# A recurrent-attention, two-MLP kernel: its first MLP group in float32 worked per chunk of 128 tokens, its bonus vector loaded by rows, its step order recomputed

## The chip, the cores and the metric

The kernel runs on one core of one Trainium2 chip. The metric is the device time in microseconds (us) of one execution; 359.74 us is the median of three runs of the kernel before (359.56 to 360.32). One execution was also taken with the hardware profiler; its trace is what the rows below come from.

## What is computed

The reference, cut to its three stages. `r`, `k`, `v`, `w` are [2, 8, 768, 48], all float32:

```python
def _attn_ref(r, k, v, w, u):              # recurrence over t, per batch and head
    for t in range(S):
        cur = einsum('bhd,bhe->bhde', u * k[t], v[t])
        y[t] = einsum('bhd,bhde->bhe', r[t], state + cur)
        state = w[t][..., None] * state + einsum('bhd,bhe->bhde', k[t], v[t])

def _moe_ref(x, g_ln, w_ch1, w_ch2):       # x: [2, 768, 384]; w_ch1 384x1536, w_ch2 1536x384
    xn = (x - mean) / sqrt(var + 1e-06) * g_ln
    return x + maximum(xn @ w_ch1, 0) @ w_ch2

def _moe2_ref(x, w_in, w_spatial, b_spatial, w_out):
    h = maximum(x @ w_in, 0); u, v = halves of h
    v_s = einsum('ts,bsd->btd', w_spatial, layer_norm(v)) + b_spatial[None, :, None]
    return (u * v_s) @ w_out
```

The weights arrive as float64, and the kernel makes float32 of them on the chip.

## The kernel before

The 768 tokens of each of the two batches are cut into 6 chunks of 128, so there are 12 chunks, numbered i = 2c + b. Each chunk goes through the attention in chunked form: `prep` (decay scans and products on VectorE), `keys_t` (transposed keys), `scores`, `values`, `state`, `norm` (layer norm statistics, a ScalarE square root, a normalized `xn`), and `turned`, which transposes `x` and `xn` and copies them out of PSUM: `x` to `x2v`, `xn` to `xfirst` (float32) for chunks 0 and 1, and to a float16 high part and low part in a ring (`xring_h`, `xring_l`) for the others.

The first MLP works on groups of two chunks, 256 token columns: `moe1(g)` for g = 0 to 5. For each of the 12 slices f of 128 hidden units, `up(f)` multiplies the weights `w1` with the 256 columns, ScalarE applies the relu (`hi`), and `down(f)` multiplies `w2` into three accumulators. Group 0 uses the float32 weights `w1f` and `w2f` directly. Groups 1 to 5 use float16 high and low parts (`w1h`, `w1l`, `w2h`, `w2l`) in three products each. The 24 weight pieces (`w1_piece`, `w2_piece`, 384 KB of float64 words each) are loaded on SP's queue, and each needs a shift, a rebias on ScalarE, a sign step and a merge on VectorE (`convert`, lines 549 to 608, the merge being line 590) before it is `w1f` or `w2f`; the copy to the high part and the subtraction for the low part come later. After the attention, stage 2 (`v_tile`, `u_tile`, `sp_tile`, `o_tile`) computes the second MLP.

Every instruction is a step `add(engine, cost, key, fn, r, w)`. A planner inside the kernel (class `Plan`) runs a list schedule over these steps with the costs written there: whenever an engine is free, it takes the ready step with the lowest key. The result is a fixed order of instructions for each engine. The keys come from the constants in `PP` (line 56). So `PP` decides the order, and at run time each engine goes through its own list in order and waits at any instruction whose input isn't there. Where the planner sees TensorE waiting it puts in matmuls on a zero tile, `pw<-warm`, which compute nothing that is used. It does so only up to the first step that writes the PSUM bank `acc0`, which is a `down` of group 0.

PSUM banks are handed out in rotation by tag (`bank(tag)`): two banks for `up`, two for `acc`. Where a helper issues every operation, all have its line: `mm` is line 394, `cp` line 385, `sub` 388, `mul` 391.

The bonus vector `u` of 384 numbers is also needed as `ud`, [112, 8], one column per head, with the 48 values of the head down the partitions. `set_ud` clears it on GpSimd, and `load_u` (line 525) fills it with two DMAs that pick single elements of `u`. They stand on SP's queue between the token loads of chunk 0 and chunk 1.

Of the kernel before, what the change touches and what calls it, by code (L numbers as in the profile page):

```python
# [8 lines left out]
F32 = mybir.dt.float32  # L9
# [12 lines left out]
DM = H * D  # L22
# [320 lines left out]
@with_exitstack  # L343
def tile_rwkv_moe_gmlp(ctx: ExitStack, tc: tile.TileContext, dt_in, tok_in, vg_in, u_in, g_in, w1_in, w2_in, win_in, wsp_in, b_in, wout_in, out, plan_only=False):
    nc = tc.nc
# [124 lines left out]
    def load_d(i, key):  # L470
        c, b = divmod(i, B)
        s = i % 2

        def part(lo, hi, first):
            def fn():
                if first:
                    t["dt", i] = a2.tile([R, DTC], F32, tag=f"dt{i % 2}", name=f"dt{i}")
                Q.dma_start(out=t["dt", i][:, lo:hi], in_=dt_in[b, c, :, lo:hi])  # L478
            return fn

        if i < B:
            for n, (lo, hi, w) in enumerate(((2 * NP * C, DTC, "dw"), (NP * C, 2 * NP * C, "dk"), (0, NP * C, "dr"))):
                add("D", 750, key + 0.01 * n, part(lo, hi, not n), w=[(w, s)])
        else:
            add("D", 2250, key, part(0, DTC, True), w=[("dw", s), ("dk", s), ("dr", s)])

    def load_k(i, key):
        c, b = divmod(i, B)
        n = DM if i < NU else 3 * DM

        def fn():
            k = t["tk", i] = share.tile([128, 3 * DM], F32, tag=f"tk{i % 2}", name=f"tk{i}")
            Q.dma_start(out=k[:, 0:n], in_=tok_in[b, c, :, 0:n])

        add("D", 640 * n // DM, key, fn, w=[("tv", i % 2), ("tr", i % 2)])

# [37 lines left out]
    add("G", 508, -80, set_mask, w=["mask"])  # L534
    add("G", 42, -95, set_ud, w=["ud"])
    for b in range(B):
# [205 lines left out]
    def scores(i):  # L742
        s = i % 2
        pp = [bank("sc"), bank("sc")]
        ams = [slot("am", AB), slot("am", AB)]

        def sc():
            q_ = [pst(pp[j], f"sc{i}_{j}") for j in range(2)]
            t["sc", i] = q_
            for pr in range(NP):  # L750
                for j, (lo, hi) in enumerate(halves):
                    mm(q_[j][:, C * pr:C * pr + C], t["kt", i][lo:hi, pr], t["rt", i][lo:hi, pr], True, True)

# [6 lines left out]
        add("T", 1090, ka(i, "sc"), sc, r=[("E", s), ("G", s), "att"], w=pp, use=0.42)  # L760
        for j in range(2):
            add("V", cv(512), ka(i, "am"), masked(j), r=[pp[j], "mask", "att"], w=[ams[j]], two=False)
        t["amt", i] = ams

    def values(i):
# [168 lines left out]


    def moe1(g):
        o = (B * g) % RING * C
        n = B * C
        qs = [(B * g + j) % RING for j in range(B)]
        xr = [(a, q) for a in (("xh", "xl") if g else ("xf",)) for q in qs]  # L940
        xh, xl = xring_h[:, :, o:o + n], xring_l[:, :, o:o + n]
# [6 lines left out]
        def up(f):  # L948
            sl = slice(128 * f, 128 * f + 128)
            p = bank("up")  # L950
            hh, hl = slot("hh" if g else "hf", 3), slot("hl", 3) if g else None
            hts[f] = hh, hl

            def mm_():
                z = t["up", g, f] = pst(p, f"pup{g}_{f}_")
                if not g:
                    for k in range(KD):
                        mm(z[:, 0:n], w1f[:, k, sl], xfirst[:, k], k == 0, k == KD - 1)
                    return
                mm3(z[:, 0:n], [(w1h[:, k, sl], w1l[:, k, sl], xh[:, k], xl[:, k]) for k in range(KD)])  # L960

            def hi():
                hs[f] = [hp.tile([128, n], F16 if g else F32, tag=f"{hh[0]}{hh[1]}", name="hh")]
                A.activation(out=hs[f][0], in_=t["up", g, f][:, 0:n], func=ACTF.Relu)
# [4 lines left out]

            add("T", 9 * ch(256) if g else 3 * 430, ku(g, f), mm_, r=[*([("w1h", f), ("w1l", f)] if g else [("w1", f, "f")]), *xr], w=[p])  # L970
            add("A", ca(256, True), ku(g, f) - PP["EV"], hi, r=[p], w=[hh])
            if not g:
                hts[f] = (hh,)
                return
            add("V", cv(256), ku(g, f) - PP["EV"], lo, r=[p, hh], w=[hl], two=False)

        def down(f):
            def mm_(d):
                def fn():
# [3 lines left out]
                    sl = slice(128 * d, 128 * d + 128)  # L983
                    first, last = f == 0 and d != 1, f == KH - 1 and d > 0
                    if not g:
                        mm(acc(d), w2f[:, f, sl], hs[f][0], first, last)
                        return
                    hh, hl = hs[f]
                    mm3(acc(d), [(w2h[:, f, sl], w2l[:, f, sl], hh, hl)], start=first, stop=last)
                return fn  # L990

            for d in range(KD):
                w = at if f == 0 and d == 0 else [at[d // 2]]
                add("T", 3 * ch(256) if g else 430, ku(g, f + 1) + 0.01, mm_(d), r=[*([("w2h", f), ("w2l", f)] if g else [("w2", f, "f")]), *hts[f]], w=w)
# [7 lines left out]
        xv = x2v.rearrange("q k (b c t) -> q k b c t", b=B, t=C)[:, :, :, g]  # L1002
        k = ku(g, KH) - PP["EV"]
        x2 = [("x2", B * g + j) for j in range(B)]

        def plus(z, y):
            V.scalar_tensor_tensor(out=z, in0=y, scalar=W_UP ** -2, in1=z, op0=ALU.mult, op1=ALU.add)

        add("V", cv(512), k, lambda: plus(xv[:, 0:2], t["acc", g, 0].rearrange("q (k b t) -> q k b t", k=2, b=B)), r=[at[0]], w=x2, two=False)
        add("V", cv(256), k, lambda: plus(xv[:, 2], acc(2).rearrange("q (b t) -> q b t", b=B)), r=[at[1]], w=x2, two=False)  # L1010

# [6 lines left out]
    for i in range(NCH + 1):  # L1018
# [12 lines left out]
        if i == 1:  # L1031
            t["pwt"] = bank("acc")
            for f in range(KH):
                key = PP["CV"] + PP["CS"] * f
                for j, piece in enumerate((w1_piece, w2_piece)):
                    n = 2 * f + j
                    piece(f, (key + PP["CW"] * j, 0.01), lo_eng="V", sh=who("SH", n), sg=who("SG", n), later=PP["HK"] + PP["HS"] * f + PP["HW"] * j)
        if i >= 2 and i % 2 == 0:
            moe1(i // 2 - 1)
    T2 = mstart(NC)  # L1040
# [309 lines left out]
def _pack(r, k, v, w, u, moe_g_ln, moe_w_ch1, moe_w_ch2, moe2_w_in, moe2_w_spatial, moe2_b_spatial, moe2_w_out):  # L1350
# [48 lines left out]
```

## Time and profile before

| what | us |
|---|---|
| median of 3 runs | 359.74 |
| the profiled execution, its own time | 362.65 |
| its span, first to last instruction | 360.9 |
| TensorE busy (matmuls, filler included) | 351.7 |
| of that, filler `pw<-warm`, 259 matmuls | 19.0 |
| VectorE busy | 283.6 |
| ScalarE busy | 155.3 |
| mean granted TensorE clock, share of full speed | 0.991 |

PE is TensorE, PEld its weight loads, DVE VectorE, ACT ScalarE, POOL GpSimd, SP SyncE, whose queue (SPq) issues the DMAs. A matmul's shown duration includes its latency, and matmuls overlap; what one costs in a full stream is read from the distance between starts. A float32 matmul shows as two instructions. `pup` is the PSUM tile that `up` writes, numbered anew for each f.

### The profile page before, as it was taken

To read this page: it belongs to the slowest core of one execution; us is meant where nothing else is said; L and a number is where in the kernel's file an instruction comes from. 1 tells how busy PE (TensorE), PEld (TensorE's weight loads), DVE (VectorE), ACT (ScalarE), POOL (GpSimd) and SP (SyncE) were. 2 spreads that over 40 slices of the span, in tenths; PEclk is the share of its full clock that TensorE was granted. 3 is DMA by queue.
4 is the path that set the end of the run, shared out by engine and by line. 5 is a ranking of instruction groups with operands and counts; after the bars stand their busy time and mean duration, and the time that the engine had idled before them with its cause. 6 is when DMAs were issued, how large, how long until landed. Compare 5 with 4: busy or idle time off the path is not lost.

```text
span 360.9 us, 7549 instructions
## 1 busy us (share of the span) xinstructions
PE 351.7 (97%) x3041; PEld 298.8 (83%) x3041; DVE 283.6 (79%) x675; ACT 155.3 (43%) x364; POOL 2.2 (1%) x22
## 2 busy tenths in 40 slices
PE   8989999999999999999999999999999999999992
PEld 8989887779888888888889888889765899965692
DVE  7969999999999999999999999999255783025500
ACT  1557988333232332423544765663421354211121
POOL 1000000000000000000000000000000000000000
PEclk9989999999999999999999999999999999999998
DMA  8999796132222541320101026601000000210021
GB/s 211 295 307 360 232 312 201 33 112 67 77 67 78 145 129 41 119 67 31 59 31 60 30 74 200 194 3 44 3 2 0 2 0 2 79 54 2 0 84 58
DMA packets 13022, 34.85 MB, mean 97 GB/s; under 512 B 1840, under 2 KB 3888, under 8 KB 12976
## 3 DMA queue, kind: packets, MB, share of 16 engines
q1 hardware_dynamic: 12976, 34.26, 30.4%
q8 instruction: 26, 0.43, 0.5%
q14 instruction: 20, 0.16, 0.1%
HBM read 31.90 MB, written 2.36 MB: 95 GB/s over the span
## 4 chain that ended last, share of the span: by engine, by line
PE 89%; DMA 7%; ACT 1%; SPq 1%; issue 0%; DVE 0%; ACTq 0%
PE p L394 34%; PE acc L394 21%; DMA raw<-in_w 5%; PE sc L394 3%; DMA tk<-in_tok 2%; PE kT L717 1%; SPq L478 1%; PE pup__641 L394 0%; PE y__996 L394 0%; PE pup__930 L394 0%; PE pup__804 L394 0%; PE pup__1051 L394 0%; PE pup__981 L394 0%; PE pup__845 L394 0%; PE pup__773 L394 0%; PE pup__750 L394 0%
## 5 line engine op out<-in xcount | busy, mean ns | idle before, releaser
L394 PE MATMUL acc<-hh,w2h 128*128 128x256 f16 x180 | 49.2, 273 | 0.0
L394 PE MATMUL acc<-hl,w2h 128*128 128x256 f16 x180 | 49.1, 273 | 0.0
L394 PE MATMUL acc<-hh,w2l 128*128 128x256 f16 x180 | 49.1, 273 | 0.0
L394 PE MATMUL p<-ws,vn 128*128 128x384 f16 x288 | 47.1, 326 | 0.0
L394 PEld LDWEIGHTS <-vn 128*128 128x128 f16 x288 | 28.0, 98 | 18.7 <-issue 0.4
L394 PEld LDWEIGHTS <-w2h 128*128 128x128 f16 x360 | 33.9, 98 | 6.3 <-issue 2.2
L394 PEld LDWEIGHTS <-w1h 128*128 128x128 f16 x360 | 34.9, 98 | 4.3 <-issue 0.2
L1224 DVE SCALAR_TENSOR_TENSOR misc<-p,misc 128x384 f32<-128x384 f32 x16 | 8.9, 558 | 30.6 <-PE p L394 30.6
L385 ACT ACTIVATE gh<-misc 128x384 fp32r<-128x384 f32 x16 | 8.4, 523 | 41.2 <-DVE misc L1225 41.2
L568 ACT ACTIVATE raw<-raw 128x384 f32<-128x384 f32 (+1 forms) x40 | 20.8, 524 | 4.3 <-DMA raw<-in_w 4.3
L574 ACT ACTIVATE raw<-raw 128x384 uint32<-128x384 uint32 (+1 forms) x31 | 15.9, 512 | 11.9 <-DMA raw<-in_w 11.9
L585 DVE SCALAR_TENSOR_TENSOR raw<-raw 128x384 int32<-128x384 int32 (+1 forms) x40 | 20.2, 511 | 0.4 <-ACT raw L568 0.3
L394 PE MATMUL pw<-warm 128*128 128x128 f16 x259 | 19.0, 242 | 1.1 <-DVE warm L499 1.1
L394 PEld LDWEIGHTS <-w2l 128*128 128x128 f16 x180 | 17.6, 98 | 2.1
L394 PEld LDWEIGHTS <-w1l 128*128 128x128 f16 x180 | 17.6, 98 | 2.1
L394 PEld LDWEIGHTS <-warm 128*128 128x128 f16 x259 | 18.0, 111 | 1.2 <-DVE warm L499 1.1
L394 PE MATMUL acc<-hh,w2f 128*128 128x256 f32 x72 | 17.9, 385 | 0.0
L388 DVE TENSOR_TENSOR gl<-misc,gh 128x384 fp32r<-128x384 f32 x16 | 8.9, 558 | 9.4 <-ACT gh L385 9.4
L394 PE MATMUL p<-woh,gl 128*128 128x384 f32 x48 | 16.3, 340 | 0.0
L394 PE MATMUL p<-woh,gh 128*128 128x384 f32 x48 | 16.2, 337 | 0.0
L394 PE MATMUL p<-xh,winh 128*128 128x384 f32 x48 | 16.2, 337 | 0.0
L394 PE MATMUL p<-wol,gh 128*128 128x384 f32 x48 | 16.1, 336 | 0.0
(702 smaller groups left out, 911.4 us busy)
## 6 DMA issues: line engine op xcount, KB each, us to landing
raw<-in_w SPq DMA_DIRECT2D x24, 384.0 KB, 7.2
dt<-in_dt SPq DMA_DIRECT2D x10, 675.5 KB, 5.3
tk<-in_tok SPq DMA_DIRECT2D x10, 576.0 KB, 3.7
raw<-in_win SPq DMA_DIRECT2D x12, 256.0 KB, 3.1
raw<-in_wsp SPq DMA_DIRECT2D x6, 384.0 KB, 3.4
out<-misc SPq DMA_DIRECT2D x12, 192.0 KB, 1.9
raw<-in_wout SPq DMA_DIRECT2D x4, 384.0 KB, 3.4
dt<-in_dt SPq DMA_DIRECT2D x4, 224.0 KB, 5.2
```

Of the source, the lines that this page charges most:

```text
L385: A.activation(out=out, in_=in_, func=ACTF.Copy)
L388: eng[e].tensor_tensor(out=out, in0=in0, in1=in1, op=ALU.subtract)
L394: T.matmul(out=out, lhsT=lhsT, rhs=rhs, start=start, stop=stop)
L478: Q.dma_start(out=t["dt", i][:, lo:hi], in_=dt_in[b, c, :, lo:hi])
L568: A.activation(out=e, in_=e, func=ACTF.Copy, scale=REBIAS * 2 if whole else REBIAS)
L574: A.activation(out=z, in_=z, func=ACTF.Copy, scale=TOP3, bias=TOP3_BIAS)
L585: V.scalar_tensor_tensor(out=lw, in0=hw, scalar=SIGN, in1=lw, op0=ALU.bitwise_and, op1=ALU.bitwise_or)
L717: T.transpose(pv[:, j, 0:R], t["kt", i][:, j], ident[0:R, 0:R])
L1224: add("V", cv(384), key, lambda: V.scalar_tensor_tensor(out=tm_(), in0=t["spp", b, th, f][:, 0:384], scalar=1.0 / S_UP, in1=t["b"][:, ts], ...
```

## The change

- `moe0` takes the place of `moe1(0)`. Its `up(f, j)`, its relu and its three `down(f, j)` are done for each of the two chunks j on 128 columns, where `moe1(0)` did both on 256. `up(f, j)` needs only `xfirst` of chunk j. The two chunks add into the same accumulators. The relu results have four buffers (`hf`), where they had three. As `bank("up")` is called for j = 0 and j = 1 in turn, each chunk has one of the two `up` banks. The steps for j = 0 have keys of their own (`E0`, `E0S`), which are lower than nearly all others.
- `moe1(g)` for g = 1 to 5 issues the same instructions as before.
- `ud` comes laid out as [112, 8] from the host (`in_ud`) in one DMA. The two DMAs of `load_u` by single elements and the clearing on GpSimd go.
- The costs that the planner is told change for some loads and matmuls, and all constants of `PP` that set keys change. The order on every engine is computed anew from them. `SH` moves three of the 24 shift steps of the weight pieces from VectorE to ScalarE.

The core of the diff:

```diff
-PP = {'SK': 12.413, ... 'T0': 18.217, 'P': 68.821, 'H': 29.796, ... 'M0': -20.127, 'M0S': 16.711, 'AH': 55.305, 'AG': -2.079, 'US': 6.83, 'EV': 33.376, 'CV': 3.765, 'CS': 12.226, 'CW': 3.915, 'WK': 602.422, ... 'SH': 'AAVVVAVAAVAVAVVVA', ...}
+PP = {'SK': 19.856, ... 'T0': 7.113, 'P': 66.66, 'H': 9.065, ... 'M0': -27.066, 'E0': -4.31, 'E0S': -20.7, 'M0S': 18.835, 'AH': 54.981, 'AG': -36.101, 'US': 7.041, 'EV': 1006.671, 'CV': -7.511, 'CS': 17.627, 'CW': 7.82, 'WK': 938.724, ... 'SH': 'AVAAVAVVAAAVAVA', ...}
...
-                add("D", 750, key + 0.01 * n, part(lo, hi, not n), w=[(w, s)])
+                add("D", 800, key + 0.01 * n, part(lo, hi, not n), w=[(w, s)])
...
-    def set_ud():
-        G.memset(ud, 0.0)
...
     def load_u():
-        uv = u_in.rearrange("(p two d) -> two d p", two=2, d=D)
-        for a, (lo, hi) in enumerate(halves):
-            Q.dma_start(out=ud[lo:lo + D, a::2], in_=uv[a])
+        Q.dma_start(out=ud, in_=ud_in)
...
+    def moe0():
+        at = [bank("acc"), bank("acc")]
+        def key(f, j):
+            return ku(0, f) if j else T0 + PP["E0"] + PP["E0S"] * f
+        def up(f, j):
+            p, h = bank("up"), slot("hf", 4)
+            def mm_():
+                z = t["up", f, j] = pst(p, f"pup0_{f}_{j}_")
+                for k in range(KD):
+                    mm(z[:, 0:C], w1f[:, k, 128 * f:128 * f + 128], xfirst[:, k, C * j:C * j + C], k == 0, k == KD - 1)
+            def hi():
+                t["h", f, j] = hp.tile([128, C], F32, tag=f"hf{h[1]}", name="hh")
+                A.activation(out=t["h", f, j], in_=t["up", f, j][:, 0:C], func=ACTF.Relu)
+            add("T", 3 * 216, key(f, j), mm_, r=[("w1", f, "f"), ("xf", j)], w=[p])
+            add("A", ca(C, True), key(f, j) - PP["EV"], hi, r=[p], w=[h])
+            return h
+        def down(f, j, h):
+            def mm_(d):
+                def fn():
...
+                    mm(t["acc", 0, d // 2][:, o:o + C], w2f[:, f, 128 * d:128 * d + 128], t["h", f, j], (f, j) == (0, 0) and d != 1, (f, j) == (KH - 1, B - 1) and d > 0)
+                return fn
+            for d in range(KD):
...
+                add("T", 216, key(f + 1, j) + 0.01, mm_(d), r=[("w2", f, "f"), h, ...], w=[("sum", d // 2, j), *w])
+        for f in range(KH):
+            for j in range(B):
+                down(f, j, up(f, j))
+        added(0, at, *[[("sum", q, j) for j in range(B)] for q in range(2)])
...
         if i >= 2 and i % 2 == 0:
-            moe1(i // 2 - 1)
+            moe1(i // 2 - 1) if i > 2 else moe0()
```

`added` holds the two VectorE additions into `x2v` that stood at the end of `moe1`.

## Rows read from the trace of the kernel before

**Rows 1.** The longest of TensorE's three waits in the whole span: total us, times, longest.

```profile
PE xnT__510 L918 <- ACT xn L907: 1.3, 1, 1.3
```

**Rows 2.** Stretches: length, busy us PE, PEld, DVE, ACT, POOL, PEclk, DMA share, GB/s.

```profile
33.13:354.31 321.18, 321.10 (x2651) 269.18 (x2650) 256.16 (x613) 139.58 (x330) 0.57 (x10) 1.00 0.25 78
12.00:33.00 21.00, 19.58 (x254) 18.57 (x251) 17.82 (x46) 12.89 (x31) 0.00 (x0) 0.92 1.00 315
33.00:79.00 46.00, 46.00 (x358) 38.03 (x356) 44.14 (x101) 32.90 (x81) 0.00 (x0) 1.00 0.61 196
79.00:242.00 163.00, 163.00 (x1655) 141.00 (x1653) 158.88 (x379) 71.71 (x178) 0.57 (x10) 1.00 0.27 81
242.00:361.00 119.00, 112.23 (x645) 90.28 (x642) 53.28 (x134) 35.59 (x75) 0.00 (x0) 0.99 0.07 25
```

**Rows 3.** The filler `pw` alone by stretch: length, PE busy, PEclk, DMA share, GB/s.

```profile
25.00:30.00 5.00, 2.83 (x49) 1.00 0.96 318
...
35.00:60.00 25.00, 0.00 (x0) 1.00 0.80 255
```

**Rows 4.** TensorE in order of time, 17 to 36 us: start, duration, instruction.

```profile
17.46 1.07 PE L394 MATMUL y__372<-tk,am 128*128 128x48 f32 x8
18.46 1.44 PE L394 MATMUL sc<-E,Gs 64*128 64x128 f32 x16
...
25.01 0.50 PE L918 MATMUL xT__497<-ident,x 128*128 128x128 f32 x3
25.34 0.44 PE L394 MATMUL pw<-warm 128*128 128x128 f16 x5
...
34.38 1.46 PE L394 MATMUL pup__654<-xfirst,w1f 128*128 128x256 f32 x6
35.68 0.59 PE L394 MATMUL acc<-hh,w2f 128*128 128x256 f32 x2
```

**Rows 5.** ScalarE in order of time, 23 to 36 us.

```profile
23.63 0.55 ACT L574 ACTIVATE raw<-raw 128x384 uint32<-128x384 uint32 x1 [2.19 <-DMA raw<-in_w]
24.51 0.29 ACT L877 ACTIVATE sd<-k_var,eps_t 128x1 f32<-128x1 f32 x1
...
27.62 0.49 ACT L385 ACTIVATE xfirst<-xnT__510 128x384 f32<-128x384 f32 x1 [0.27 <-PE xnT__510 L918]
...
30.75 0.57 ACT L574 ACTIVATE raw<-raw 128x384 uint32<-128x384 uint32 x1 [0.75 <-DMA raw<-in_w]
...
32.44 0.49 ACT L385 ACTIVATE xfirst<-xnT__620 128x384 f32<-128x384 f32 x1 [0.18 <-PE xnT__620 L918]
```

**Rows 6.** VectorE in order of time: chunk 0's statistics, merges of `w2f`, chunk 4's first scan.

```profile
21.19 0.17 DVE L876 BATCH_NORM_AGGREGATE k_var<-st 128x2 f32<-128x6 f32 x1
...
33.31 0.55 DVE L590 SCALAR_TENSOR_TENSOR w2f<-raw 128x384 int32<-128x384 int32 x1
...
37.48 0.53 DVE L590 SCALAR_TENSOR_TENSOR w2f<-raw 128x384 int32<-128x384 int32 x1
...
48.57 0.56 DVE L590 SCALAR_TENSOR_TENSOR w2f<-raw 128x384 int32<-128x384 int32 x1
...
65.36 1.23 DVE L635 TENSOR_TENSOR_SCAN Gs<-dt,onehot 112x516 f32<-112x516 f32 x1
```

**Rows 7.** Chain that ended last: the `acc` of f = 4, and the first `pup` of group 1.

```profile
46.20 1.29 PE acc L394 x6
...
78.84 1.09 PE pup__1148 L394 x9
```

**Rows 8.** The relu of `pup__654` and VectorE's last step ahead of group 1.

```profile
35.88 0.38 ACT L964 ACTIVATE hh<-pup__654 128x256 f32<-128x256 f32 x1
77.62 0.55 DVE L388 TENSOR_TENSOR xring_l<-xnT__1118,xring_h 128x384 f16<-128x384 f32 x1
```

**Rows 9.** Granted clock around a stretch of short matmuls (columns as in Rows 2).

```profile
20.00:22.00 2.00, 2.00 (x29) 1.91 (x27) 2.00 (x7) 0.77 (x2) 0.00 (x0) 0.50 1.05 405
```

**Rows 10.** DMA issues: KB each, median us to landing.

```profile
ud<-in_u SPq DMA_DIRECT2D x2, 0.8 KB, 5.6
```

More of the change, by code (lines that the diff above doesn't have):

```diff
@@ L482, in load_d @@
             for n, (lo, hi, w) in enumerate(((2 * NP * C, DTC, "dw"), (NP * C, 2 * NP * C, "dk"), (0, NP * C, "dr"))):
-                add("D", 750, key + 0.01 * n, part(lo, hi, not n), w=[(w, s)])
+                add("D", 800, key + 0.01 * n, part(lo, hi, not n), w=[(w, s)])
         else:
-            add("D", 2250, key, part(0, DTC, True), w=[("dw", s), ("dk", s), ("dr", s)])
+            add("D", 2500, key, part(0, DTC, True), w=[("dw", s), ("dk", s), ("dr", s)])
     def load_k(i, key):
@@ L493, in fn @@
             Q.dma_start(out=k[:, 0:n], in_=tok_in[b, c, :, 0:n])
-        add("D", 640 * n // DM, key, fn, w=[("tv", i % 2), ("tr", i % 2)])
+        add("D", 700 if n == DM else 1900, key, fn, w=[("tv", i % 2), ("tr", i % 2)])
     def set_hot():
@@ L758, in masked @@
             return fn
[L760 removed]
+        add("T", 1200, ka(i, "sc"), sc, r=[("E", s), ("G", s), "att"], w=pp, use=0.42)
         for j in range(2):
@@ L932, in turned, with plus, added @@
         add("V", cv(DM), ka(i, "xnT"), lambda: sub("V", xring_l[:, :, o:o + C], pv("xn"), xring_h[:, :, o:o + C]), r=[pn, ("xh", q)], w=[("xl", q)], two=False)
+    def plus(z, y):
+        V.scalar_tensor_tensor(out=z, in0=y, scalar=W_UP ** -2, in1=z, op0=ALU.mult, op1=ALU.add)
+    def added(g, at, r0=(), r1=()):
+        xv = x2v.rearrange("q k (b c t) -> q k b c t", b=B, t=C)[:, :, :, g]
+        k = ku(g, KH) - PP["EV"]
+        x2 = [("x2", B * g + j) for j in range(B)]
+        add("V", cv(512), k, lambda: plus(xv[:, 0:2], t["acc", g, 0].rearrange("q (k b t) -> q k b t", k=2, b=B)), r=[at[0], *r0], w=x2, two=False)
+        add("V", cv(256), k, lambda: plus(xv[:, 2], t["acc", g, 1][:, 0:256].rearrange("q (b t) -> q b t", b=B)), r=[at[1], *r1], w=x2, two=False)
@@ L948, in up @@
         def up(f):
-            sl = slice(128 * f, 128 * f + 128)
             p = bank("up")
-            hh, hl = slot("hh" if g else "hf", 3), slot("hl", 3) if g else None
-            hts[f] = hh, hl
+            hh, hl = hts[f] = slot("hh", 3), slot("hl", 3)
             def mm_():
                 z = t["up", g, f] = pst(p, f"pup{g}_{f}_")
[L956 to L960, printed above, removed]
+                mm3(z[:, 0:n], [(w1h[:, k, 128 * f:128 * f + 128], w1l[:, k, 128 * f:128 * f + 128], xh[:, k], xl[:, k]) for k in range(KD)])
             def hi():
-                hs[f] = [hp.tile([128, n], F16 if g else F32, tag=f"{hh[0]}{hh[1]}", name="hh")]
+                hs[f] = [hp.tile([128, n], F16, tag=f"hh{hh[1]}", name="hh")]
                 A.activation(out=hs[f][0], in_=t["up", g, f][:, 0:n], func=ACTF.Relu)
@@ L983, in fn @@
                     sl = slice(128 * d, 128 * d + 128)
[L984 to L987, printed above, removed]
                     hh, hl = hs[f]
-                    mm3(acc(d), [(w2h[:, f, sl], w2l[:, f, sl], hh, hl)], start=first, stop=last)
+                    mm3(acc(d), [(w2h[:, f, sl], w2l[:, f, sl], hh, hl)], start=f == 0 and d != 1, stop=f == KH - 1 and d > 0)
                 return fn
@@ L1000, in moe1 @@
                 down(f - 1)
[L1002 to L1010, printed above, removed]
+        added(g, at)
     def loads(i):
@@ L1367, in _pack @@
     tok = np.concatenate([tmajor(v), tmajor(r), tmajor(k)], axis=3)
+    uh = np.asarray(u).reshape(NP, 2, D)
+    ud = np.zeros((R, H), uh.dtype)
+    for a in range(2):
+        ud[64 * a:64 * a + D, a::2] = uh[:, a].T
     def words(x):
```

27 lines of the change are left out of this document (15 added, 12 removed).

## The prediction, made blind

> **What bounds the kernel now.** I read four views in turn. The waits of TensorE come first: there are three, and the longest is one of 1.3 us for the normalized tokens of chunk 0 [rows 1]. The stretches say that none comes late [rows 2]: from 33.13 to 354.31 it is busy for 321.10 of 321.18 us at the full granted clock. But until 33 us part of its work is filler: 2.83 us of the five from 25 to 30, and none from 35 on [rows 3]. So the time is the moment at which real work begins for good, about 33.1 us, plus 321.2 us of matmuls, plus 6.6 us of a last copy and store. Only fewer or cheaper matmuls, or an earlier start, can shorten it.
>
> What holds the start? TensorE's first matmul of group 0 goes at 33.1 (1.30 us ahead of `pup__654`) [rows 4], right behind the copy of chunk 1's `xfirst`, which ends at 32.93 [rows 5]. Chunk 0's `xfirst` was there at 28.11 [rows 5]. So 5 us pass in which one chunk is ready and its partner isn't. Ahead of that, VectorE had chunk 0's variance at 21.36 [rows 6], but its square root starts on ScalarE only at 24.51, since ScalarE stood for 2.19 us at the shift of a weight piece whose DMA hadn't landed [rows 5].
>
> The other engine to watch is VectorE: 44.14 us busy of the 46 from 33 to 79, and 158.88 of the 163 that follow, but 53.28 of 119 in the last stage [rows 2].
>
> **The change part by part.**
>
> *Price of the split.* Six float32 passes of 256 columns take 1.30 us (from 34.38 to 35.68), so 217 ns each; group 0 has 144 of them, 31.2 us [rows 4]. The change makes 288 passes of 128 columns. From below they cost 108 ns each, the same in all; less is excluded, as the same columns stream through. From above, eight passes of 48 columns with 128 columns of weights take 1.00 us, 125 ns each [rows 4], which makes 36.0 us, 4.8 more. The nearest row is the three float32 transposes that load 128 columns of weights and stream 128: 0.33 us, 110 ns each [rows 4]. I take that: 31.7 us, **+0.5**, with 0 and 4.8 as ends.
>
> *The earlier start.* Chunk 0 needs 3.6 us from the start of its square root to the end of its `xfirst` copy (24.51 to 28.11) [rows 5]. If the new order takes ScalarE off the waiting shift, the copy ends at about 21.4 + 3.6 = 25.0; if not, at 28.1. I take the middle, 26.5. Chunk 1 comes 3 to 5 us behind. A slice f is 1.3 us of TensorE for one chunk, 2.6 for both. From 26.5 to 33.1 there are 6.6 us. The relu of the first slices has nothing to hide behind: `pup__654` ends at 35.68, its relu at 36.26, so about 0.6 us each time [rows 4, 8], and the weights of slice 3 come only at 33.86 [rows 6]. So I count slices 0 to 2 of chunk 0 (3.9 us) and about a slice of chunk 1: **5.0 us** of real work ahead of 33.1, with 2.0 (chunk 0 at 28.1, chunk 1 as before) and 6.6 as ends.
>
> *Whether the weights keep up.* From 12 to 33 us the DMA share is 1.00 at 315 GB/s [rows 2]: weight pieces come as fast as they can. `w2f` of slices 3, 4 and 8 is merged at 33.86, 38.01 and 49.13 [rows 6]. Slices 0 to 3 are 10.4 us of TensorE. With 5.0 done, the rest lasts from 33.1 to 38.5, and slice 4 is there at 38.0. From then on a slice takes 2.6 us and a merge comes each 2.8 us: at slice 8 TensorE is at 48.9 and the merge at 49.1. So the weights just carry a head start of 5.0, and cap it near 5.5 as long as they come as now. (Before, `down(4)` runs at 46.20, 8 us behind its merge [rows 6, 7]; that lead is what is used up.) Bringing loads forward can raise the cap only by holding back those of chunks 2 and 3.
>
> *Whether VectorE passes it on.* Group 1 can't start before the low part of chunk 3, which VectorE finishes at 78.17; TensorE follows at 78.84 [rows 7, 8]. For the gain to live VectorE must be there 4 us sooner. Its idle time is 3.2 us from 12 to 33 and 1.9 from 33 to 79 [rows 2]; and it spends several us from 65.36 on with the preparation of chunk 4 [rows 6], which group 1 doesn't need. By the old constants chunk 4's key is 198.6 + 68.8 - 55.3 - 29.8 = 182.3, ahead of group 1's first `up` at 198.6. By the new ones it is 206.1 + 66.7 - 55.0 - 9.1 = 208.7, behind 206.1. So I expect that work to be put behind and the gain to pass. In the groups after that VectorE has 4.1 us idle, and 65.7 us in the last stage, to which range reductions can move [rows 2].
>
> *What hides.* Twelve more relus and three more shifts on ScalarE: at most 12 x 0.38 + 3 x 0.57 = 6.3 us, at least 1.7 (half-width relus at no fixed cost) [rows 5, 8]; 13.1 us of idle ScalarE from 33 to 79 cover it [rows 2]. Without that cover each would sit in TensorE's way. VectorE loses three shifts. Each chunk now has a single `up` bank, so `up(f+1, j)` waits for the relu of `up(f, j)`, about 0.6 us; one `down` of 0.65 us covers it, and the other chunk's step as well. I take **+0.3**, between 0 and 24 x 0.6 = 14.4 if nothing covered. The `ud` load: two DMAs of 0.8 KB that land after 5.6 us [rows 10] become one. That is nothing beside the megabytes on full engines; what it delays is a single issue on SP's queue, so I take 0, up to 0.5 gained if the weights behind it start sooner.
>
> *Sum.* -5.0 + 0.5 + 0.3 = **-4.2 us**. The profiled execution took 362.65 (span 360.9), so it would become 358.4. The median of the runs stands 2.9 us below that execution; carried to it, 359.74 - 4.2 = **355.5**.
>
> **The rivals.**
>
> *VectorE takes it back* (about no change). If chunk 4's work stays where it is, only the 1.9 us of idle time between 33 and 79 can be won, less 0.8 of costs, and the constants may lose that again: 358.6 to 360.5, say 359.6. For it: the 44.14 of 46. Against it: the new keys.
>
> *TensorE runs slow in the head start.* The filler ends with the first `down` of group 0, which now comes some 8 us sooner, before the weights have a lead. From 20 to 22 us the granted clock was 0.50, the lower of its two levels, 1.2 GHz, behind a stretch of short matmuls in which TensorE was busy [rows 9]. If work in pieces of 0.65 us with waits between them does the same, half of the 5.0 is lost: 359.74 - 2.5 + 0.8 = 358.0. The Trainium skill, "TensorE: Matmul & The Clock Gate", section "HAM oscillation — how this bites in real kernels", says that bursts of matmuls shorter than the DMA waits between them start at the lower clock each time. By that rule the time would be this rival's; the row agrees that the clock falls here, but no run shows it for waits on weights.
>
> *Slower.* Without filler and with ScalarE in order, a shift that waits for its DMA (2.19 and 0.75 us in [rows 5]) also holds the relus queued behind it, and TensorE has one bank for each chunk, so it stands. The place is 26 to 50 us. Before, TensorE had nothing to lose there until 33. If the new order makes eight such waits of 1 us behind the point where TensorE is the bound, the price is 8.0: 359.74 - 4.2 + 8.0 = 363.5. It decides from 4.2 us of such waits on.
>
> *The change doesn't do what it says.* If `xfirst` of chunk 0 comes no sooner than 32 us in the new order, the costs alone remain: 360.5.
>
> *More.* If the planner also gets weights ahead of the loads of chunks 2 and 3, the cap goes, and chunk 0 at 25.0 makes up to 8 us: 359.74 - 8.0 + 0.8 = 352.5.
>
> **How the numbers follow.** Forecast (353.5 to 358) 0.48; more 0.12; VectorE 0.14; slow clock 0.07; nothing done 0.06; slower 0.13. Two runs of this kernel can be told apart from about 0.2%, 0.7 us. Faster by more than that: forecast, more, nearly all of the slow clock and a third of the VectorE case, 0.70. Within it: most of the VectorE case and of nothing done, 0.13. Slower: 0.17. The range leaves out the slower case and the far end of "more": 351 to 361. It takes in the upper end of the split's price (355.5 + 4.3 = 359.8) and the head start of 2.0 (358.5).
>
> **What would show it.** Right: `pup` of chunk 0 begins at 25 to 28 us, 128-column passes 110 ns apart, filler below 19.0 us by about 5, group 1 starting near 74.5, and TensorE without waits from there. Wrong: waits of TensorE for `hh` or for `w1f` and `w2f` that add up to over 4 us between 26 and 50 (slower); a group 1 that still starts near 78 behind `xring_l` (VectorE); passes 125 ns apart (split price); a granted clock of 0.5 beyond 26 us (slow clock). A trace with those steps right and new waits past 79 us would show a cause that I don't have here.

## The result

Run side by side, the kernel after takes 357.78 us (median of 20 runs, 356.43 to 359.53) and the kernel before 361.05 (median of 20, 359.56 to 364.88): a ratio of 0.990 [0.9877, 0.9923], so faster by 1.0%. The forecast was 355.5, the range 351 to 361. In a second comparison, among the experiments, the same kernel stands at 0.9947 [0.9918, 0.9977]; the gain is 0.5 to 1%, 2 to 3.5 us by these ratios (3.3 and 1.5 us between the medians).

The profiled execution after took 359.14 (span 357.4), 3.5 us less than that of before (362.65, span 360.9). Its waits of TensorE (total us, times, longest), which answer to [rows 1]:

```profile
PE pup__595 L394 <- ACT hh L956: 1.5, 1, 1.5
PE pw L394 <- DVE warm L499: 1.1, 1, 1.1
PE sc L394 <- DVE E L391: 0.3, 1, 0.3
PE y__387 L394 <- DVE am L751: 0.2, 1, 0.2
```

The wait for chunk 0's normalized tokens is gone; a new one of 1.5 us, for a relu, stands in its place. The stretches, which answer to [rows 2, 9]:

```profile
20.00:22.00 2.00, 2.00 (x38) 1.82 (x38) 2.00 (x9) 2.00 (x6) 0.00 (x0) 1.00 1.04 364
12.00:33.00 21.00, 19.24 (x229) 17.76 (x227) 19.14 (x50) 14.96 (x37) 0.00 (x0) 1.00 1.03 311
33.00:79.00 46.00, 45.73 (x472) 42.94 (x472) 45.09 (x103) 34.62 (x93) 0.00 (x0) 1.00 0.55 182
79.00:242.00 163.00, 162.91 (x1664) 140.25 (x1662) 157.45 (x372) 70.84 (x177) 0.57 (x10) 1.00 0.29 86
242.00:361.00 119.00, 109.16 (x626) 87.23 (x624) 52.00 (x133) 34.27 (x72) 0.00 (x0) 0.99 0.07 25
```

From 33 to 242 us TensorE is nearly as full as before (45.73 us of the 46 from 33 to 79, with the wait of 0.3), and it has 109.16 us left at 242 where it had 112.23. So what was gained was gained before 79 and kept. The filler alone (length, TensorE busy, clock, DMA share, GB/s), first after and then before:

```profile
0.00:40.00 40.00, 14.59 (x210) 1.00 0.93 285
```

```profile
0.00:40.00 40.00, 19.01 (x259) 0.96 0.93 287
```

That closes the sum for these two executions. TensorE is busy 348.0 us in all against 351.7: 4.4 less filler, 0.7 more real work. Its idle time is 9.4 against 9.2. Together -4.4 + 0.7 + 0.2 = -3.5.

Where the early start comes from is seen on ScalarE, from 20 to 34 us, which answers to [rows 5]:

```profile
20.17 0.28 ACT L871 ACTIVATE sd<-k_var,eps_t 128x1 f32<-128x1 f32 x1
...
24.05 0.48 ACT L385 ACTIVATE xfirst<-xnT__511 128x384 f32<-128x384 f32 x1
...
29.47 0.56 ACT L562 ACTIVATE raw<-raw 128x384 f32<-128x384 f32 x1 [1.87 <-DMA raw<-in_w]
29.93 0.25 ACT L956 ACTIVATE hh<-pup__577 128x128 f32<-128x128 f32 x1
30.09 0.28 ACT L871 ACTIVATE sd<-k_var,eps_t 128x1 f32<-128x1 f32 x1
...
33.57 0.49 ACT L385 ACTIVATE xfirst<-xnT__631 128x384 f32<-128x384 f32 x1 [0.50 <-PE xnT__631 L912]
```

Chunk 0's square root no longer stands behind a waiting shift: 20.17 instead of 24.51, and its `xfirst` is there at 24.53 instead of 28.11. But at 29.47 the shift of another piece has waited 1.87 us for its DMA, with a relu and chunk 1's square root queued behind it. That relu is TensorE's 1.5 us, and chunk 1's `xfirst` ends at 34.06, later than before (32.93).

TensorE in order of time, 25 to 40 us, which answers to [rows 4]:

```profile
25.83 0.91 PE L394 MATMUL pup__551<-xfirst,w1f 128*128 128x128 f32 x6
...
27.11 0.94 PE L394 MATMUL pup__577<-xfirst,w1f 128*128 128x128 f32 x6
27.88 0.83 PE L394 MATMUL acc<-hh,w2f 128*128 128x128 f32 x6
30.24 0.94 PE L394 MATMUL pup__595<-xfirst,w1f 128*128 128x128 f32 x6 [1.52 <-ACT hh L956]
31.01 0.83 PE L394 MATMUL acc<-hh,w2f 128*128 128x128 f32 x6
31.68 0.86 PE L394 MATMUL pup__613<-xfirst,w1f 128*128 128x128 f32 x6
32.37 0.83 PE L394 MATMUL acc<-hh,w2f 128*128 128x128 f32 x6
...
38.08 0.83 PE L394 MATMUL pup__698<-xfirst,w1f 128*128 128x128 f32 x6
38.75 0.83 PE L394 MATMUL pup__705<-xfirst,w1f 128*128 128x128 f32 x6
39.42 0.83 PE L394 MATMUL acc<-hh,w2f 128*128 128x128 f32 x6
```

By 33.1 us, where group 0 began before, seven pieces of chunk 0 are done (`up` of slices 0 to 3, `down` of slices 0 to 2). The starts at 38.08, 38.75 and 39.42 show one piece: 0.67 us for six passes, 112 ns each. At the other end, in VectorE's order of time [rows 6, 8]:

```profile
70.04 0.56 DVE L388 TENSOR_TENSOR xring_l<-xnT__1129,xring_h 128x384 f16<-128x384 f32 x1
...
74.19 1.22 DVE L629 TENSOR_TENSOR_SCAN Gs<-dt,onehot 112x516 f32<-112x516 f32 x1
```

Chunk 3's low part starts at 70.04 instead of 77.62, and chunk 4's first scan has moved behind it, from 65.36 to 74.19. Group 1's first `up` begins at 71.29 (before 78.77 on the timeline).

### The profile page after: what moved, and what is told of

It reads as the page before. It is cut to its first block, busy times and chain, and to the rows that moved or that the text cites. A ratio compares the mean times of both kernels' runs of the same rounds, so it can differ in the third digit from the quotient of the medians.

```text
span 357.4 us, 7751 instructions
## 1 busy us (share of the span) xinstructions
PE 348.0 (97%) x3136; PEld 299.0 (84%) x3136; DVE 283.4 (79%) x672; ACT 157.1 (44%) x379; POOL 2.2 (1%) x21
## 4 chain that ended last, share of the span: by engine, by line
PE 87%; DMA 6%; DVE 4%; issue 1%; SPq 0%; ACT 0%; ACTq 0%; DVEq 0%
PE p L394 34%; PE acc L394 20%; DMA raw<-in_w 5%; PE sc L394 3%; DMA dt<-in_dt 1%; DVE raw L579 1%; PE kT L711 1%; DVE E L642 1%; DVE E L391 0%; PE y__2689 L394 0%; PE y__2178 L394 0%; PE y__1507 L394 0%; PE y__1318 L394 0%; PE y__1907 L394 0%; PE y__2784 L394 0%
## 5 line engine op out<-in xcount | busy, mean ns | idle before, releaser
L568 ACT ACTIVATE raw<-raw 128x384 uint32<-128x384 uint32 (+1 forms) x34 | 17.6, 518 | 9.6 <-DMA raw<-in_w 9.4
L394 PE MATMUL acc<-hh,w2f 128*128 128x128 f32 x144 | 20.2, 277 | 0.0
L394 PEld LDWEIGHTS acc<-hh,w2f 128*128 128x128 f32 x144 | 17.9, 192 | 0.4 <-issue 0.2
L394 PE MATMUL p<-xh,winl 128*128 128x384 f32 x48 | 16.1, 335 | 0.0
```

The lines of the kernel that those rows point to most:

```text
L394: T.matmul(out=out, lhsT=lhsT, rhs=rhs, start=start, stop=stop)
L568: A.activation(out=z, in_=z, func=ACTF.Copy, scale=TOP3, bias=TOP3_BIAS)
```

## The experiments

After the result my theory was: the split brings 4.7 us of early start and costs 1.0; the gain lives because the order puts chunk 4's work behind chunk 3's on VectorE. The rival: the new order brings the gain and the split little. Each kernel below has the planner work out its order anew from the steps and keys of that kernel. Each ratio is to the kernel before in the same comparison.

### The order alone

The kernel after with group 0 in 256 columns, by `moe1` as before (its float32 branch is back).

```diff
-            moe1(i // 2 - 1) if i > 2 else moe0()
+            moe1(i // 2 - 1)
```

> The changed kernel with group 0 put back to 256 columns: new constants, new order and the new ud load stay, only the split is gone. If the gain is the head start of chunk 0, it is gone here: group 0 has to wait for chunk 1's xfirst, which the changed kernel has at 34.06 us against 32.93 before, so 0 to 1.5 us slower than the kernel before (ratio 1.000 to 1.004), with filler back near 19 us. If the new order alone carries the gain (rival), ratio near 0.990 as for the whole change.

Measured: 361.51 us, ratio 1.003 [1.0002, 1.0058], span 359.7, as foreseen. Chunk 0's `xfirst` copy starts at 24.19, as early as after, but group 0 starts at 32.85. The filler is 20.04 us, and from there on TensorE is full. So the order brings nothing by itself. Against this kernel the split is worth about 1% (0.990 or 0.9947 over 1.003).

### The split alone

The kernel before with `moe0` and the two keys that it needs; all other constants as before.

```diff
-            moe1(i // 2 - 1)
+            moe1(i // 2 - 1) if i > 2 else moe0()
```

> The kernel before with nothing but the split of group 0 (keys of chunk 0 by the two new constants; old constants otherwise, old ud load). If the head start is what counts, chunk 0's work fills some of the 5 us between the two xfirst copies of before (28.1 and 32.9): about 3 us of matmuls moved ahead, less about 1 us for the price of 128 columns: 1 to 2.5 us faster, ratio 0.993 to 0.997. If the order carries the gain, this one only pays the price of the split: +0.5 to +1.0 us, ratio 1.001 to 1.003.

Measured: 363.82 us, ratio 1.0085 [1.0051, 1.0118]. Both numbers missed: the split alone makes the kernel slower. Its waits of TensorE and two stretches:

```profile
PE xnT__1162 L918 <- ACT xn L907: 1.6, 1, 1.6
PE pw L394 <- DVE warm L499: 1.1, 1, 1.1
...
70.00:75.00 5.00, 3.82 (x43) 3.46 (x39) 4.67 (x15) 1.62 (x4) 0.00 (x0) 1.00 0.73 227
75.00:80.00 5.00, 4.62 (x43) 3.48 (x44) 5.00 (x12) 1.47 (x4) 0.00 (x0) 0.69 0.11 31
```

The early start is there (`pup__537` at 26.8, filler 1.78 us of the five from 25 to 30). It is lost at 70 to 80 us: group 0 runs out (the last pass of its `down` starts at 72.5), chunk 3 isn't ready (`xring_l` at 76.99), TensorE waits for chunk 3's normalized tokens, and then its clock is 0.69. Chunk 4's scan stands at 63.21, ahead of chunk 3. That fitted my theory of chunk 4, so I tested it. The spans of the two profiled executions, 361.2 here and 360.9 before, are nearly the same: the trace shows where a head start of 4.8 us of filler (14.24 against 19.01) was lost again, but only 0.3 of the 3 us by which the runs are slower.

### Chunk 0 held back

The kernel after, but each `up` waits for both chunks' `xfirst`.

```diff
-            add("T", 3 * 216, key(f, j), mm_, r=[("w1", f, "f"), ("xf", j)], w=[p])
+            add("T", 3 * 216, key(f, j), mm_, r=[("w1", f, "f"), ("xf", 0), ("xf", 1)], w=[p])
```

> The changed kernel, but each up of group 0 waits for xfirst of both chunks, so that the split is kept and its head start is not. Head start theory: no gain, the price of the split on top of e1: 0.5 to 2.5 us slower than the kernel before, ratio 1.001 to 1.007, and group 0's first matmul at about 34. Against e1 it gives the price of the split: +0.5 us by 110 ns a pass, +1.0 us by 112 ns. If the order carries the gain: ratio 0.990 to 0.993.

Measured: 368.98 us, ratio 1.0246 [1.0197, 1.0296]. The start is at 32.44 (about 34 foreseen) and the filler 20.42 us, so the head start is gone as meant; but the ratio lies outside all that was foreseen. The order falls apart at 75 to 85 (TensorE 3.38 us busy in 75:80, with a wait of 1.4 us for `E` of chunk 4; then clock 0.69, and chunk 3's `xring_l` only at 80.05), so it doesn't give the price of the split by itself.

### The old load of `ud`

The kernel after with the two DMAs by elements and the clearing.

```diff
-        Q.dma_start(out=ud, in_=ud_in)
+        uv = u_in.rearrange("(p two d) -> two d p", two=2, d=D)
+        for a, (lo, hi) in enumerate(halves):
+            Q.dma_start(out=ud[lo:lo + D, a::2], in_=uv[a])
...
+    add("G", 42, -95, set_ud, w=["ud"])
```

> The changed kernel with the old ud load: two DMAs by single elements and the clearing on GpSimd. If the load by rows is worth nothing, the time is that of the whole change, ratio 0.990, within 0.002. If it carries part of the gain by letting the weights start sooner (up to 0.5 us in the prediction), ratio 0.991 to 0.992; if it carries most, over 0.995.

Measured: 358.2 us, ratio 0.9951 [0.9921, 0.9982], just past the 0.995 that was to mean that the load carries most of the gain. But the kernel after itself, run once more below in another comparison, stands at 0.9947, and its medians (357.78 and 358.78) lie on both sides of 358.2. So no worth of the new layout of `ud` is seen, though the two kernels never ran side by side.

### Chunk 4 put behind in the split alone

The keys of chunks 4 and 5 are raised, and with them their steps on every engine.

```diff
-        return mstart(g) - PP["AH"] - (1 - j) * H_ + (PP["AG"] if g == 1 else 0)
+        return mstart(g) - PP["AH"] - (1 - j) * H_ + (PP["AG"] if g == 1 else 27.0 if g == 2 else 0)
```

> The kernel before with the split of group 0 (as in e2), and one thing more: the keys of chunks 4 and 5 are raised by 27, so that VectorE's preparation of chunk 4 stands behind the last steps of chunk 3 and not ahead. If e2 lost its head start because VectorE was at chunk 4 when group 1 needed chunk 3's low part (ready at 77.5 us in e2, 70.6 in the changed kernel), that part comes near 72 here, the granted clock stays at 1.00 from 75 to 80, and the time is 1.5 to 3.5 us below the kernel before: ratio 0.990 to 0.996. If other constants carry it, the ratio stays near e2's, 1.004 to 1.010.

Measured: 367.08 us, ratio 1.0206 [1.0157, 1.0254]. Chunk 4's scan went to 75.47, as meant, but chunk 3's `xring_l` stayed at 76.61. And TensorE no longer has chunk 4's attention to fill the time ahead of group 1:

```profile
PE xnT__1137 L918 <- ACT xn L907: 2.4, 1, 2.4
PE pup__581 L394 <- ACT hh L962: 1.3, 1, 1.3
PE pup__1149 L394 <- DVE xring_l L388: 1.2, 1, 1.2
...
70.00:75.00 5.00, 2.61 (x22) 2.15 (x20) 4.75 (x16) 1.29 (x3) 0.00 (x0) 0.97 0.36 120
75.00:80.00 5.00, 3.22 (x16) 2.11 (x15) 5.00 (x11) 0.87 (x2) 0.00 (x0) 0.50 0.00 0
```

My theory of chunk 4 fell: moving its work alone does not bring chunk 3 forward.

### Chunk 4 brought forward in the kernel after

The keys of chunks 4 and 5 are lowered, again on every engine.

```diff
-        return mstart(g) - PP["AH"] - (1 - j) * H_ + (PP["AG"] if g == 1 else 0)
+        return mstart(g) - PP["AH"] - (1 - j) * H_ + (PP["AG"] if g == 1 else -27.0 if g == 2 else 0)
```

> The changed kernel with the keys of chunks 4 and 5 lowered by 27, so that chunk 4's preparation stands ahead of group 1 again, as in the kernel before. If the head start lives only when VectorE puts chunk 4 behind, chunk 3's low part is late again and the gain goes: ratio 0.998 to 1.005. If the order of chunk 4 doesn't matter, 0.989 to 0.992 as in the changed kernel.

Measured: 364.44 us, ratio 1.0095 [1.0059, 1.0131], outside both. Chunk 3 comes little later (71.65), but group 1's first `up` only at 78.22: attention steps of chunks 4 and 5 stand ahead of it, and of the last steps of group 0 as well, whose `down` ends only here:

```profile
88.21 1.29 PE L394 MATMUL acc<-hh,w2f 128*128 128x128 f32 x10
```

TensorE waits 1.1 us for `Gs` and 1.2 us up to `k_var` on VectorE. So the place of chunks 4 and 5 does matter in this order, but not by making chunk 3 late, as I had expected.

### The waiting shift put behind

In the kernel after, ScalarE's shifts of pieces 7 to 9 wait for chunk 1's normalized tokens (`r=behind`), so that no relu stands behind them.

```diff
-                    piece(f, (key + PP["CW"] * j, 0.01), lo_eng=who("LO", n), sh=who("SH", n), sg=who("SG", n), later=PP["HK"] + PP["HS"] * f + PP["HW"] * j)
+                    piece(f, (key + PP["CW"] * j, 0.01), lo_eng=who("LO", n), sh=who("SH", n), sg=who("SG", n), later=PP["HK"] + PP["HS"] * f + PP["HW"] * j, behind=[("xn", 1)] if n in (7, 8, 9) else ())
```

> The changed kernel, with shift and rebias of three weight pieces (w2 of slice 3, both of slice 4) put behind chunk 1's xn, so that ScalarE doesn't stand at a piece that hasn't landed while a relu and chunk 1's square root are queued behind it (1.87 us at 27.6 to 29.5 in the changed kernel; TensorE waits 1.5 us for that relu). If this wait is a loss at the end, TensorE's wait is gone, chunk 1's xfirst comes near 31 and not 34, and the time is 1.0 to 1.5 us below the changed kernel: ratio 0.986 to 0.988. If the weights cap the head start anyway, it is the same as the changed kernel: 0.989 to 0.992; if delayed pieces leave TensorE without weights later, more.

Measured: 365.1 us, ratio 1.0145 [1.0105, 1.0185]. This lies above all that was foreseen for a gain or for no change. The early wait is gone (TensorE busy 4.97 us of 25:30), but a wait of 1.0 us for chunk 1's `xfirst` stands at 33.13; that copy ends at 33.1, not near 31. Chunk 3 has slipped to 74.36, TensorE waits 1.5 and 0.6 us for `xring_l` and `xring_h`, and the clock in 75:80 is 0.70.

### The kernel after, once more

> The changed kernel itself beside these three on the same chip, as their measure, and for e4: ratio 0.990, between 0.988 and 0.993; its own median is 357.8. If it comes to 0.993 to 0.995 here, the old ud load of e4 (0.995) is no loss; if it stays at 0.988 to 0.991, the load by rows is worth 1 us.

Measured: 358.78 us, ratio 0.9947 [0.9918, 0.9977], span 357.2. That is not the 0.990 of the first comparison but the other case, in which the old `ud` load is no loss. The wait of 1.5 us for the relu isn't there: the shift at 29.27 starts with no wait for its DMA. But the clock of 20:22 is 0.50 here, chunk 0's `xfirst` copy starts at 26.00 instead of 24.05, and the filler is 16.24 us instead of 14.59. From the relu of `pup__595` on (31.27 us in the first execution, 31.26 here) the two run within 0.1 us of each other, and their spans differ by 0.2 us. So the 2 us by which chunk 0 was ready sooner in the first were spent there waiting for the weight piece, and the wait of 1.5 us is no fixed cost of the change.

### What the losing kernels share

So far each kernel that lost more than 0.5% has TensorE idle between 65 and 85 us, so I set the traces side by side: the start of the last pass of `down` of group 0, the end of chunk 3's `xring_l`, TensorE's idle time from 65 to 85 us, and its clock from 75 to 80.

| kernel | last pass of `down`, group 0 | chunk 3 ready | idle 65:85 | clock 75:80 | ratio |
|---|---|---|---|---|---|
| before | 74.9 | 78.17 | 0.00 | 1.00 | 1 |
| after | 72.8 | 70.60 | 0.00 | 1.00 | 0.990, 0.9947 |
| order alone | 74.0 | 73.68 | 0.00 | 1.00 | 1.003 |
| split alone | 72.5 | 77.54 | 1.81 | 0.69 | 1.0085 |
| after, chunk 0 held back | 75.3 | 80.60 | 1.62 | 0.97 | 1.0246 |
| split, chunk 4 behind | 71.7 | 77.15 | 4.16 | 0.50 | 1.0206 |
| after, chunk 4 early | 89.8 | 72.20 | 3.62 | 1.00 | 1.0095 |
| after, shift behind | 71.7 | 74.89 | 2.48 | 0.70 | 1.0145 |

Before, chunk 4's attention fills the time from the end of group 0 to group 1's first `up`:

```profile
75.22 1.16 PE L394 MATMUL sc<-E,Gs 64*128 64x128 f32 x16
...
78.77 0.28 PE L394 MATMUL pup__1148<-xring_h,w1h 128*128 128x256 f16 x1
```

In after and in the order alone chunk 3 is ready before group 0 ends. In the split alone, with chunk 4 behind and with the shift behind, TensorE gets to the end of group 0 3 to 5.5 us before chunk 3 is ready. With chunk 4 early it is the other way round, and with chunk 0 held back the wait is one for chunk 4; so these two lost in another way. New theory for the rest: the due time of chunk 3, that is the key that all its steps go by, decides (141.2 in the constants of before, behind all weight pieces but the last; 115.0 in those of after, between them). Two kernels tell it apart from the rest of the constants, one each way.

### The due times of chunks 2 and 3 alone, in the split alone

```diff
-        return mstart(g) - PP["AH"] - (1 - j) * H_ + (PP["AG"] if g == 1 else 0)
+        if g == 1:
+            return 114.9 - (1 - j) * 9.065
+        return mstart(g) - PP["AH"] - (1 - j) * H_
```

> The kernel before with the split, as in e2_split_only, and with the planner's due times of chunks 2 and 3 alone moved to those of the kernel after (105.8 and 114.9 instead of 111.4 and 141.2), everything else as in e2. Theory (the head start is lost at 70 to 85 us because chunk 3's x comes too late for group 1): xring_l of chunk 3 lands at 69 to 73 us instead of 77, the granted clock in 75:80 stays above 0.95, and the ratio to the kernel before is 0.988 to 0.997. Rival (the gap comes from something else in the old order, such as which weight pieces stand between): xring_l of chunk 3 moves but TensorE still idles over 1 us somewhere in 65:85, ratio 1.003 to 1.012.

Measured: 363.37 us, ratio 1.0086 [1.0054, 1.0119]. Chunk 3's `xring_l` starts at 75.78, hardly sooner than in the split alone (76.99); VectorE again has chunk 4's scans (63.52, 67.66) ahead of it, and TensorE idles 3.61 us in 65:85, at the full clock. That is the rival: the due times of chunks 2 and 3 alone are not enough.

### The due time of chunk 3 raised in the kernel after

```diff
-        return mstart(g) - PP["AH"] - (1 - j) * H_ + (PP["AG"] if g == 1 else 0)
+        return mstart(g) - PP["AH"] - (1 - j) * H_ + (PP["AG"] if g == 1 else 0) + (26.0 if (g, j) == (1, 1) else 0)
```

> The kernel after with the due time of chunk 3 alone raised by 26 us to what the kernel before has. Theory (chunk 3's x decides): xring_l of chunk 3 at 74 us or later, TensorE idle 1 to 4 us in 70:80, granted clock below 0.9 in one stretch of 75:85, ratio to the kernel before 1.002 to 1.015. Rival (chunk 3 is not what decides): ratio 0.988 to 0.996, as the kernel after.

Measured: 365.41 us, ratio 1.0127 [1.0095, 1.0159], as the theory said. The timeline of TensorE and the stretches that hold it:

```profile
70.36 1.53 PE L394 MATMUL acc<-hh,w2f 128*128 128x128 f32 x12
73.18 0.55 PE L912 MATMUL xnT__1154<-ident,xn 128*128 128x128 f32 x3 [1.29 <-ACT xn L901]
74.31 0.33 PE L394 MATMUL pup__1164<-xring_h,w1h 128*128 128x256 f16 x1 [0.58 <-ACT xring_h L385]
75.39 0.37 PE L394 MATMUL pup__1164<-xring_l,w1h 128*128 128x256 f16 x1 [0.75 <-DVE xring_l L388]
```

```profile
70.00:71.90 1.90, 1.89 (x17) 1.70 (x15) 1.90 (x9) 0.72 (x3) 0.00 (x0) 1.00 0.24 94
71.90:74.00 2.10, 0.55 (x3) 0.38 (x4) 2.10 (x6) 0.85 (x2) 0.00 (x0) 1.00 0.00 0
74.00:76.00 2.00, 0.94 (x5) 0.52 (x5) 2.00 (x6) 0.25 (x1) 0.00 (x0) 0.60 0.00 0
76.00:78.00 2.00, 2.00 (x11) 1.67 (x10) 2.00 (x3) 0.38 (x1) 0.00 (x0) 0.50 0.00 0
78.00:80.00 2.00, 2.00 (x12) 1.22 (x9) 2.00 (x6) 0.59 (x2) 0.00 (x0) 0.50 0.00 0
80.00:82.00 2.00, 2.00 (x20) 1.84 (x21) 2.00 (x6) 0.34 (x1) 0.00 (x0) 0.70 0.91 278
```

Group 0 is done at 71.9 and chunk 3 isn't. TensorE works 1.5 of the next 4.1 us, and then runs at the lower of its two clocks, 1.2 GHz, until about 81. The span is 7.0 us above that of after. TensorE's busy time is 352.4 instead of 348.0, 4.4 more: 0.8 of that is filler (15.4 against 14.6), and 3.6 is the same work taking longer; the stretches above account for about 3.0 of it (0.94 x 0.4 + 4.0 x 0.5 + 2.0 x 0.3). The remaining 2.6 us is idle time. So these gaps cost more than their length.

### The late slices in one matmul

The kernel after with its steps and keys as they are, so in the same order; from slice 5 on the places of chunk 0 are left empty, and those of chunk 1 do 256 columns.

```diff
+            n, o = (B * C, 0) if f >= 5 else (C, C * j)
...
+                if n > C and j == 0:
+                    return
...
-                    mm(z[:, 0:C], w1f[:, k, 128 * f:128 * f + 128], xfirst[:, k, C * j:C * j + C], k == 0, k == KD - 1)
+                    mm(z[:, 0:n], w1f[:, k, 128 * f:128 * f + 128], xfirst[:, k, o:o + n], k == 0, k == KD - 1)
```

> The kernel after in its own order, but from slice 5 on both chunks of group 0 go through in one matmul of 256 columns, at the place of chunk 1; chunk 0's places are left empty. 168 passes of 112 ns (18.8 us) become 84 of 217 ns (18.2 us). Theory A (price of the split alone): 0.6 us less than the kernel after, ratio to the kernel before 0.986 to 0.993. Theory B (chunk 0's slices are also cover while chunk 1 and the attention lag): the empty places turn into TensorE idle of 1 us or more between 40 and 75 us, ratio 0.994 to 1.005.

Measured: 362.93 us, ratio 1.006 [1.0031, 1.009]. Theory B, and a little beyond its upper end:

```profile
PE y__930 L394 <- DVE am L751: 1.5, 1, 1.5
PE kT L394 <- DVE tk L391: 1.2, 1, 1.2
...
55.00:60.00 5.00, 3.53 (x45) 2.66 (x43) 4.45 (x13) 4.65 (x12) 0.00 (x0) 0.83 0.88 326
```

The 0.6 us of cheaper passes is lost in waits for chunk 2's attention steps, and behind them the clock is 0.83 from 55 to 65. The slices of chunk 0 that stood between those steps were their cover. So the split does a second thing: it makes pieces that are ready early and can be put into gaps.

### All slices in one matmul, same order

The same with `f >= 0`: no early start and no price of the split.

> The kernel after in its own order, but all 12 slices of group 0 in matmuls of 256 columns at the places of chunk 1: no head start, no price of the split. Theory (head start 4.7 us, price 1.0 us): 3.7 us slower than the kernel after, filler 18 to 20 us, first up pass at 32 to 35 us, ratio to the kernel before 0.998 to 1.004. Rival (the new order brings the gain and the split nothing): ratio 0.988 to 0.994. Rival (the order without chunk 0's slices leaves TensorE idle): over 1.006.

Measured: 366.25 us, ratio 1.0175 [1.0129, 1.022]. That is the third case, TensorE left idle; the start of 33.11 was foreseen, the filler wasn't (15.8 us). TensorE in order of time:

```profile
26.99 0.33 PE L394 MATMUL pw<-warm 128*128 128x128 f16 x3
31.63 0.55 PE L912 MATMUL xnT__596<-ident,xn 128*128 128x128 f32 x3 [4.30 <-ACT xn L901]
...
33.11 2.75 PE L394 MATMUL pup__616<-xfirst,w1f 128*128 128x256 f32 x6
...
36.88 1.56 PE L394 MATMUL pup__651<-xfirst,w1f 128*128 128x256 f32 x6
```

```profile
34.00:36.00 2.00, 2.00 (x7) 1.21 (x7) 1.65 (x4) 0.58 (x3) 0.00 (x0) 0.58 1.01 371
```

The planner had put no filler where chunk 0's slices stood, so TensorE idles 4.3 us at 27 to 31.6. Six passes then take 2.75 us, at a granted clock of 0.57 from 32 to 34 and 0.58 from 34 to 36; six took 1.46 in the kernel before at 1.00 [rows 4]. As a price of the early start alone this kernel says too much; the clean pair for that is after and the order alone. There the split takes 5.5 us off the filler and adds 1.6 us of real work and 1.6 of idle time: 2.3 us between the spans (359.7 and 357.4). With the second execution of after it is 3.8, 0.9 and 0.4: 2.5 us.

None of these kernels beats the kernel after. One rival stays untested: its constants are a set of their own, and a change of any one key, even of one that bears on neither chunk 3 nor chunk 4, may cost as much. No kernel with such a change was run. The old `ud` load, whose two DMAs are planned anew too, left the time where it was, and in the kernel with chunk 3 late the waits that cost the time are seen to be for chunk 3.

## Why the prediction was right, and where it was not

**The bound.** Right. TensorE is full from the start of real work on, and the time changed by what happened ahead of that.

**The earlier start**, 5.0 us foreseen: seven pieces of 0.67 us, 4.7. The filler fell by 4.4 us, as foreseen by "about 5". The parts were otherwise than I put them. Chunk 0 came at 24.53, not 26.5, as the order did take ScalarE off the waiting shift: its square root starts at 20.17, 1.2 us ahead of the 21.4 that I had, and the way from there to the copy took 4.4 us, not 3.6. Filler stood in front of the first pass until 25.83. Chunk 1 came 9.5 us behind chunk 0 (at 34.06), not 3 to 5. So nothing of chunk 1 is in the 4.7, and the `up` of slice 3 of chunk 0 is. That the sum held is luck: the errors cancel.

**The price of the split**, 0.5 foreseen, is the term that was mis-sized: 112 ns a pass, not 110, so 288 x 112 = 32.2 us, 1.0 above the 31.2 of before. TensorE's real work grew by 0.7.

**Bank and relu waits**, 0.3 foreseen: 1.5 us in one execution of the kernel after, none in the other, 0.5 with the old `ud` load. The mechanism is that of the rival *slower* (a shift that waits for its DMA holds the relus behind it); it came once, not eight times, and ahead of 33.1 us, where it took from the early start.

**The weights.** Right: no wait of TensorE for `w1f` or `w2f` stands in the list after. They did hold the start, but through ScalarE, at the shift of a piece that hadn't landed. Whether they cap it near 5.5 wasn't tried.

**Whether VectorE passes it on.** The outcome was right: chunk 4 behind, chunk 3 at 70.04, group 1 at 71.29 (74.5 foreseen; part of this is that chunk 4's attention, which filled 75.22 to 78.77 on TensorE before, now stands behind group 1's start). The reason was incomplete. I gave one condition, chunk 4's work behind. Putting chunk 4 behind alone made the split worse (1.0206), moving chunks 2 and 3 alone left it where it was (1.0086), and undoing either in the kernel after loses more than the gain (1.0095, 1.0127). So in the order of after neither can be undone at no cost; with chunk 4 early, though, the loss came from its attention steps on TensorE, and not from a late chunk 3. Whether the two together would be enough in the order of before wasn't tried, and which of the constants the gain needs stays open.

**`ud`**, 0 foreseen: 0.9951 with the old load; 0.990 and 0.9947 without it, in two other comparisons.

**The sum.** -4.2 foreseen; -3.5 between the profiled executions, 1.0% or 3.6 us by the ratio of the first comparison, 0.5% or 1.9 by that of the second, which is less than half of the forecast. The median of 357.78 lies 2.3 above the forecast; 1.3 of that is the kernel before, which stood at 361.05 there and not at 359.74.

**The rivals.** The slow clock did not come into the early start: 1.00 in every stretch of 5 us from 25 to 95 in the kernel after. It came, in kernels that lost, behind gaps. By the rule of the Trainium skill that I had cited ("TensorE: Matmul & The Clock Gate", section "HAM oscillation — how this bites in real kernels": work between waits that are longer than itself starts slow each time), I had looked for it at waits on weights. The trace agrees with it at 76 us with chunk 3 late, though the waits there are for ScalarE and VectorE: 1.5 us of work among 2.6 us of gaps, and 0.50 behind them. In the split with chunks 2 and 3 early 3.6 us of gaps in 65:85 left the clock at 1.00; there the work between two waits was longer than they were (some 6 us between those of 1.28 and 1.14 us), so the rule doesn't bear on it.

My rival *slower* ended in a place that I didn't name. I had put it at 26 to 50 us, for waits on DMAs. The losses of the variants are at 70 to 85, where group 0 ends and group 1 begins, with one exception each at 55 and at 27 us, where chunk 0's slices had been taken out.

## What to carry over

Work that starts earlier is a gain only if what follows it is ready earlier too: look for the next seam downstream (here the end of group 0 and chunk 3's last step) and compare the two times there, before and after. Splitting a unit of work by its inputs costs little on the engine (here 112 ns where half of a 256-column pass is 108) and gives pieces that fill gaps elsewhere, but only in an order made for it: the split without the order was slower, the order without the split no faster. A gap on TensorE is to be priced with what the clock does behind it, not with its length alone: 2.6 us of gaps cost some 3 us more with chunk 3 late, and 3.6 us of them cost no more than their length with chunks 2 and 3 early (348 us of TensorE busy, as in the kernel after).

## What was not expected of the hardware

- Behind a gap TensorE's granted clock fell while it was busy: with chunk 3 late, 1.5 us of work in 4.1 us were followed by 4 us at 0.50 and 2 at 0.70. With chunks 2 and 3 early, and with chunk 4 early, 3.6 us of gaps, spread from 70 to 85, left it at 1.00. What decides between them was not settled.
- In two executions of one kernel a weight piece landed so that ScalarE waited 1.87 us for it, or not at all, and the clock of 20:22 was 1.00 or 0.50; the spans were 357.4 and 357.2. A single wait in one trace of the first 33 us is no evidence for its cost.
- A float32 pass of 128 columns with weights of its own takes 112 ns and one of 256 columns 217. Halving the columns nearly halves the time, so next to nothing is added for loading the weights, although weight loads run for 5.00 of the 5.00 us from 40 to 45 in the kernel after.
